# Moving score bounds, key sums and normalising products from VectorE to GpSimd, with paired value products and a changed release and load order

## The chip, the cores and the metric

The kernel runs on one core of a Trainium2 chip. The time is the device time of one execution in microseconds, as a median over several runs.

Five engines run at once, each through its own instructions in a fixed order: TensorE (PE in the profile, PEld for its weight loads), VectorE (DVE), ScalarE (ACT), GpSimd (POOL) and the sync engine (SP), which issues most DMAs.

## The reference

Two attention blocks on separate inputs of 2048 rows and width 512, 32 heads of 16, side by side in the output. Part A is softmax attention with one key and value head for all query heads. Part B is linear attention with softmax features.

```python
# A
q, k, v = x @ wq, x @ wk, x @ wv              # k and v: one head of 16
p = softmax(q_h @ k.T / 4)                    # 32 heads, 2048 x 2048
a = (p @ v) @ wo
# B
q, k, v = split(x @ wqkv)
phi = lambda t: concat(softmax(t @ w_phi), softmax(-(t @ w_phi)))
kv, z = phi(k).T @ v, phi(k).sum(rows)
b = ((phi(q) @ kv) / (phi(q) @ z + 1e-6)) @ wo
out = concat(a, b)
```

## The kernel before

Part A has 32 steps of four heads, and in each 16 tiles of keys. The exponential of a group of four 128x512 score tiles is made in one of two ways. ScalarE makes it exactly, two or three tiles at a time. Or VectorE makes it from the bits of a float16: it reads four score tiles from PSUM into int16 (`bits`, here "reads"), then adds a constant to the whole quad three times (`shift`), and TensorE sums four weighted versions. Such a quad costs VectorE four reads and three shifts.

```python
def bits():                                   # PSUM -> int16 in SBUF, 512 columns
    v.tensor_scalar(out=o, in0=ps[:, bank, :], scalar1=self.Z1, scalar2=self.Z0, op0=ALU.mult, op1=ALU.add)
def shift(t):                                 # SBUF -> SBUF, 2048 columns
    v.tensor_scalar(out=Z[:, t], in0=Z[:, 0], scalar1=256.0 * t, scalar2=None, op0=ALU.add)
```

The instructions stand in an order that a list scheduler in the kernel's own Python made when it was built. It keeps a model clock for each engine and picks the job that can start first, then by priority. On the chip that order is fixed: an engine that waits for one instruction does not go on to the next.

```python
job(("ss", st), "dve", 1.14, self.b_ssum, after=[("fe", st)], prio=1.9)          # key sums, part B
job(("on", sc), "dve", 0.60, ... finish_sc3(sc) ..., prio=1.3, after=[("rc", sc)] ...)  # normalising product, part A
job(("aq", ch), "dve", 0.60, ... absmax(QA[ch % 3]) ..., after=[("qa", ch)], prio=6)  # score bound
# (further jobs left out)
```

At the head of the kernel the sync queue is given all loads, the six transposes of part B first, then the bulk loads. It issues in order, so the first step's denominator copies (`finish_sc`, from `accS` to `denC`) stand behind all of them:

```python
for i in (1, 0): la = S.dma1(... dma_start_transpose(wT[i]) ..., deps=[la])
for c in range(4): la = self.load_xT(self.B_x, self.BxT, c, "BxT", la)
# then Bwv, Bwo, wo_pad (8 DMAs), wphi (8 DMAs); only then jobs
```

## Time and profile before

| | before |
|---|---|
| median of 3 runs | 816.45 us (814.57 to 816.78) |
| profiled run, span of its instructions | 809.98 us, 806.9 us |
| ScalarE busy | 748.5 us, 93% |
| TensorE busy | 733.9 us, 91% |
| VectorE busy | 722.3 us, 90% |
| GpSimd busy | 16.7 us, 2% |

The page's first part: each engine's busy time, its share of the span, and instructions.

```profile
span 806.9 us, 17313 instructions
PE 733.9 (91%) x7345; PEld 243.7 (30%) x7420; DVE 722.3 (90%) x1254; ACT 748.5 (93%) x690; POOL 16.7 (2%) x49
```

Three engines are nearly full, so the average does not name one limit. Three stretches do. The view by windows gives for each stretch the busy time of PE, PEld, DVE, ACT and POOL (instructions in brackets), then the granted TensorE clock, the DMA share and GB/s.

```profile
40.00:60.00 20.00, 10.35 (x103) 2.92 (x96) 10.55 (x19) 11.62 (x10) 0.00 (x0) 0.84 0.71 133
80.00:400.00 320.00, 294.64 (x3204) 97.82 (x3231) 311.50 (x538) 312.36 (x297) 4.83 (x10) 0.99 0.11 9
767.00:807.00 40.00, 28.58 (x304) 8.87 (x305) 18.55 (x35) 22.60 (x22) 0.00 (x0) 0.90 0.11 20
```

Between 80 and 400 us ScalarE works 312 of 320 us. Between 40 and 60 us it works 11.6 of 20, and so do the others: a hole. The last 40 us are half empty too. The timeline shows the hole (start, duration, engine, line, operation; in square brackets the idle time before it and what ended that):

```profile
44.92 0.68 DVE L1410 COPY f_accS<-f_ps 128x512 f32<-128x512 f32 x1
46.47 3.78 SPq L1465 DMA_DIRECT2D f_wo_pad<-in_A_wo_dram  x8
50.37 3.63 SPq L1487 DMA_DIRECT2D f_wphi<-in_B_w_phi_dram  x8
54.04 3.28 SPq L1801 DMA_DIRECT2D f_denC<-f_accS  x4
58.91 0.25 DVE L1809 RECIPROCAL f_denC<-f_denC 128x16 f32<-128x16 f32 x1 [8.52 <-DMA f_denC<-f_accS]
61.56 1.45 ACT L1653 ACTIVATE f_PT<-f_ps 128x1536 bf16<-128x1536 f32 x1 [8.52 <-PE f_ps L1598]
```

The accumulator was copied by 45.6 us, its denominators were fetched only at 54.0, because the queue was still issuing bulk loads. VectorE stood 8.5 us at the reciprocal, and in-order TensorE and ScalarE stood behind it.

The costliest groups (line, engine, operation, out<-in, shapes, count; busy us, mean ns of one; idle us before them and what ended it):

```profile
L1653 ACT ACTIVATE f_PT<-f_ps 128x1536 bf16<-128x1536 f32 (+1 forms) x621 | 721.4, 1264 | 45.3 <-PE f_ps L1598 42.1
L1745 DVE TENSOR_SCALAR f_Z<-f_ps 128x512 int16<-128x512 f32 x496 | 324.1, 682 | 34.9 <-PE f_ps L1598 34.3
L1758 DVE TENSOR_SCALAR f_Z<-f_Z 128x2048 int16<-128x2048 int16 x372 | 244.5, 685 | 0.7
```

The last two lines belong together. A shift handles 2048 columns in 685 ns, a read of PSUM 512 columns in 682. The shift runs at four times the rate.

### The profile page before, as it was taken

The page shows a single profiled execution, that of the slowest core. Times are in us where ns is not written, and L with a number is a line of the kernel's source. Part 1 is how long each engine was busy: PE and PEld are TensorE (multiplying, and loading weights), DVE is VectorE, ACT ScalarE, POOL GpSimd, SP SyncE. Part 2 cuts the span into 40 slices and gives each one's busy share as a digit, 9 for nine tenths or more (in the row PEclk, how much of TensorE's full clock was granted, in tenths as well). Part 3 has the DMA queues.
Part 4 walks back from the last instruction along what each step waited for, and adds up shares of the span by engine and source line. Part 5 has one row for each costly group of instructions (what it writes and reads, how often), then busy time and mean ns, then how long its engine had stood idle before and what let it go on. Part 6 is the DMA issues. An engine that isn't in the chain of part 4 may idle for free.

```text
span 806.9 us, 17313 instructions
## 1 busy us (share of the span) xinstructions
PE 733.9 (91%) x7345; PEld 243.7 (30%) x7420; DVE 722.3 (90%) x1254; ACT 748.5 (93%) x690; POOL 16.7 (2%) x49
## 2 busy tenths in 40 slices
PE   8959998988999999899999999999999999999894
PEld 2212322322323333323333233333333233333331
DVE  3759999999999999989899958999979999999962
ACT  4858999999999999999999998999999999999983
POOL 5000000000000000100000000000000000000000
PEclk9788999999999999999999998999999999999997
DMA  6561111101111101110101111011111101111110
GB/s 132 108 129 8 7 9 9 9 2 8 9 9 21 22 2 8 9 8 7 9 9 20 17 19 8 16 14 21 7 15 15 22 9 14 21 14 21 19 11 30
DMA packets 45179, 17.10 MB, mean 21 GB/s; under 512 B 37092, under 2 KB 43236, under 8 KB 45096
## 3 DMA queue, kind: packets, MB, share of 16 engines
q1 hardware_dynamic: 45096, 15.93, 15.8%
q8 instruction: 60, 0.98, 0.5%
q14 instruction: 23, 0.19, 0.1%
HBM read 2.15 MB, written 4.19 MB: 8 GB/s over the span
## 4 chain that ended last, share of the span: by engine, by line
DVE 63%; PE 25%; DMA 5%; ACT 2%; SPq 2%; issue 2%; DVEq 0%
DVE f_Z L1745 27%; DVE f_Z L1758 19%; PE f_ps L1598 8%; PE f_ps L1783 5%; PE f_ps L1695 4%; DMA f_AxT<-in_A_x_dram 2%; DVE f_vS L2041 2%; PE f_ps L2092 2%; ACT f_PT L1653 2%; DVE f_ssum L2015 2%; DVE f_accS L1410 2%; DMA f_BxT<-in_B_x_dram 2%; DVE f_On L1826 2%; PE f_ps L1839 2%; DVE f_Wk L2152 2%
## 5 line engine op out<-in xcount | busy, mean ns | idle before, releaser
L1653 ACT ACTIVATE f_PT<-f_ps 128x1536 bf16<-128x1536 f32 (+1 forms) x621 | 721.4, 1264 | 45.3 <-PE f_ps L1598 42.1
L1745 DVE TENSOR_SCALAR f_Z<-f_ps 128x512 int16<-128x512 f32 x496 | 324.1, 682 | 34.9 <-PE f_ps L1598 34.3
L1598 PE MATMUL f_ps<-f_QA,f_KR 32*128 32x512 bf16 x2048 | 315.6, 390 | 31.1 <-DVE f_Z L1745 20.8
L1758 DVE TENSOR_SCALAR f_Z<-f_Z 128x2048 int16<-128x2048 int16 x372 | 244.5, 685 | 0.7
L1598 PEld LDWEIGHTS f_ps<-f_QA,f_KR 32*128 32x128 bf16 x2048 | 80.3, 91 | 259.0 <-issue 85.7
L1695 PE MATMUL f_ps<-f_PT,f_VA 128*32 128x512 bf16 x1552 | 154.4, 395 | 2.6 <-DVE f_accS L1410 2.5
L1783 PE MATMUL f_ps<-f_Z,f_VK 128*32 128x512 f16 x1984 | 132.4, 388 | 3.3 <-DVE f_Z L1758 1.6
L1695 PEld LDWEIGHTS f_ps<-f_PT,f_VA 128*32 128x32 bf16 x1552 | 38.5, 93 | 97.9 <-issue 85.6
L1404 PE MATMUL f_ps<-f_ones,f_zero 128*128 128x512 bf16 (+7 forms) x204 | 61.2, 361 | 2.1 <-POOL f_zero L1423 1.3
L1783 PEld LDWEIGHTS f_ps<-f_Z,f_VK 128*32 128x32 bf16 x1984 | 42.3, 96 | 64.1 <-DVE f_Z L1758 16.7
L2092 PE MATMUL f_ps<-f_BxT,f_Wq 128*128 128x512 bf16 x112 | 29.4, 380 | 3.3 <-issue 1.6
L1839 PE MATMUL f_ps<-f_wo_pad,f_On 128*128 128x512 bf16 x87 | 22.9, 381 | 2.3 <-issue 1.1
L2152 DVE TENSOR_TENSOR f_Wk<-f_ps,f_wq 128x512 bf16<-128x512 f32 x32 | 21.9, 684 | 3.0 <-PE f_ps L2141 2.9
L1404 PEld LDWEIGHTS f_ps<-f_ones,f_zero 128*128 128x128 bf16 (+2 forms) x204 | 15.9, 97 | 28.1 <-issue 17.2
L1826 DVE TENSOR_TENSOR f_On<-f_accS,f_denS 128x512 bf16<-128x512 f32 x31 | 21.1, 682 | 0.4 <-DMA f_denS<-f_denS 0.4
L1410 DVE COPY f_accS<-f_ps 128x512 f32<-128x512 f32 x31 | 21.2, 682 | 0.2 <-PE f_ps L1695 0.2
L2041 DVE TENSOR_TENSOR f_vS<-f_ps,f_rs 128x1024 bf16<-128x1024 f32 x16 | 19.5, 1220 | 1.2 <-PE f_ps L2031 1.1
L2099 ACT ACTIVATE f_ET<-f_ps 128x512 bf16<-128x512 f32 x32 | 20.2, 636 | 0.4 <-PE f_ps L2092 0.4
L2015 DVE TENSOR_REDUCE f_ssum<-f_Ek 128x64 f32<-128x1024 bf16 x16 | 19.4, 1214 | 0.1
L1550 DVE TENSOR_SCALAR f_KR<-f_ps,f_half 128x512 bf16<-128x512 f32 x8 | 5.6, 745 | 15.1 <-PE f_ps L1542 15.1
L1588 PE MATMUL f_ps<-f_AxT,f_wq 128*128 128x512 bf16 x50 | 14.0, 393 | 4.7 <-DVE f_Z L1745 2.6
L2009 ACT ACTIVATE f_Ek<-f_ps 128x512 bf16<-128x512 f32 x32 | 17.8, 626 | 0.0
(95 smaller groups left out, 314.9 us busy)
## 6 DMA issues: line engine op xcount, KB each, us to landing
f_denS<-f_denS SPq DMA_DIRECT2D x124, 30.0 KB, 3.0
out_dram<-f_outB SPq DMA_DIRECT2D x18, 128.0 KB, 1.9
f_denC<-f_accS SPq DMA_DIRECT2D x124, 2.0 KB, 1.7
f_denS<-f_denC SPq DMA_DIRECT2D x124, 2.0 KB, 1.7
out_dram<-f_outA SPq DMA_DIRECT2D x14, 128.0 KB, 1.8
f_wq<-in_A_wq_dram SPq DMA_DIRECT2D x1, 512.0 KB, 4.2
f_Bwv<-in_B_wqkv_dram SPq DMA_DIRECT2D x1, 512.0 KB, 4.6
f_Bwo<-in_B_wo_dram SPq DMA_DIRECT2D x1, 512.0 KB, 6.8
```

The costliest lines, as they stand in the source:

```text
L1404: mm = pe.matmul(ps[0:m, bank, 0:n].rearrange("p (a n) -> p a n", n=128), lhsT=zero[0:r, 0:m], rhs=rhs, start=start, stop=start, **kw)
L1410: self.add("dve", lambda v: v.tensor_copy(out=out, in_=in_), reads=reads, writes=writes)
L1598: return pe.matmul(self.ps[:, bank, :], lhsT=self.KR[32 * g:32 * g + 32, sc % 2, kap * 128:(kap + 1) * 128], rhs=self.QA[32 * g:32 * g + 3 ...
L1653: self.add("act", lambda a: a.activation(out=PT[:, sl[0]:sl[0] + size, :], in_=ps[:, b0:b0 + size, :], func=ACT.Exp), reads=[("PS", b0 + i ...
L1695: mm = pe.matmul(ps[32 * g:32 * g + 32, bank, :], lhsT=w, rhs=PT[:, slots[g], :], start=start, stop=stop, tile_position=(0, 32 * g))
L1745: self.add("dve", lambda v: v.tensor_scalar(out=o, in0=ps[:, bank, :], scalar1=self.Z1, scalar2=self.Z0, op0=ALU.mult, op1=ALU.add), reads ...
L1758: self.add("dve", lambda v: v.tensor_scalar(out=Z[:, t], in0=Z[:, 0], scalar1=256.0 * t, scalar2=None, op0=ALU.add), reads=zk, writes=[("Z ...
L1783: mm = pe.matmul(ps[32 * g:32 * g + 32, bank, :], lhsT=w[:, k, :], rhs=Zf[:, k, sl[g], :], start=start and k == 0, stop=stop and k == 3, t ...
L1826: self.add("dve", lambda v: v.tensor_tensor(out=On[:, sc % 12, :], in0=accS[:, r, :], in1=R[:, r, :], op=ALU.mult), reads=[("accS", r), (" ...
L1839: mm = pe.matmul(ps[:, bank, :], lhsT=On[:, (8 * qc + a) % 12, q0:q0 + 128], rhs=self.wo_pad[:, a, :], start=(a == 0), stop=(a == 7))
L2092: mm = pe.matmul(ps[:, bank, :], lhsT=w[:, dc].rearrange("p x h a f -> p (x h a f)")[:, G * 128:G * 128 + 128], rhs=xT[:, dc, m * 512:(m + ...
L2152: self.add("dve", lambda v: v.tensor_tensor(out=o, in0=i, in1=w.unsqueeze(3).to_broadcast([128, 2, 16, 16]), op=ALU.mult), reads=[("PS", b ...
```

## The change

Its intent: VectorE is one of three full engines and GpSimd is idle, so give GpSimd work. Because the two engines may disturb each other, a GpSimd operation is released by the last shift of a VectorE quad (the key `lk`), and the scheduler starts it within 2 us of that. Besides: value products of ScalarE's groups run in pairs so that TensorE changes its tiling mode less often, with a higher limit of waiting groups (`HIGH` 13 to 16); the last step may take more VectorE quads (`LAST` 4, where `AHEAD`, 6, held before); the third shift of a quad now stands behind the first two; the six transposes of part B become jobs on the sync queue; two of the last four stores go to another queue. The diff, cut to its core:

```diff
-            job(("aq", ch), "dve", 0.60, ... absmax(QA ...) ...)
+            for i in range(2):      # sum of squares: product, then running sum
+                job(("aq", ch, i), "pool", 1.27, ... absmax_q(ch, i) ..., prio=6, ...)
-            job(("on", sc), "dve", 0.60, ... finish_sc3(sc) ...)
+            job(("on", sc), "pool" if sc < 29 else "dve", 1.25 if sc < 29 else 0.60, ...)
-            job(("ss", st), "dve", 1.14, self.b_ssum, after=[("fe", st)], prio=1.9)
+            for i, d in enumerate((1.27, 1.30)):      # a tree: 512, then 256, 128, 64 results
+                job(("ss", st, i), "pool", d, self.b_ssum, ...)
 # in ready(): start within LOCK of the last shift
+        if j.eng == "pool" and j.name != "kvfin" and self.asc < 32:
+            t = max(t, self.lk_from)
+            if t > self.lk_from + self.LOCK:
+                return None
 # in shift(t): the third one releases GpSimd, which reads "lk"
-                         reads=zk, writes=[("Zt", p, t)])
+                         reads=zk, writes=[("Zt", p, t)] + (["lk"] if t == 3 else []))
 # pairs of value products
-                             ok=... self.acc_ok(sc) ...
+                             ok=... self.acc_ok(sc) and self.pair(sc, q) ...
-            if j.name[0] == "pv" and self.nu - 4 * self.pvq > self.HIGH:
-                p = 0.5
+            if j.name[0] == "pv" and (self.nu - 4 * self.pvq > self.HIGH or (self.mode == "col" and j.name[1] == self.second)):
+                p = 0.5 if self.mode != "col" else 0.0
-    HIGH = 13
+    HIGH = 16
+    LOCK = 2.0
+    LAST = 4
 # late transposes
+        for i in range(6):
+            self.job(("ld", i), "sp", 0.1, ... load_late(i) ..., rel=26.0 + 5.6 * i)
 # (the third shift's dependency, buffers shared to make room, the flag's arithmetic, the stores' queue: left out)
```

More of the change, by code (lines that the diff above doesn't have):

```diff
@@ L1198, in __init__ @@
         self.wq = sb("wq", [128, 4, 512], BF)
-        self.wk_raw = sb("wk_raw", [128, 4, 16], BF)
         self.wk_rep = sb("wk_rep", [128, 4, 128], BF)
@@ L1216, in __init__ @@
         self.outA = sb("outA", [128, 2, 512], BF)
-        self.mq = sb("mq", [128, 20], F32)
+        self.mq = sb("mq", [128, 4], F32)
+        self.QM = sb("QM", [128, 512], BF)
         self.mqk = sb("mqk", [128, 4], F32)
@@ L1245, in __init__ @@
         self.wT = self.ET[:, 0:8, :]
+        self.wk_raw = self.ssum.rearrange("p a n -> p (a n)").bitcast(BF)[:, 0:64].rearrange("p (c n) -> p c n", c=4)
         self.mrow = self.Bwv[0:1, 0:2, :].rearrange("p a n -> p (a n)").bitcast(F32).rearrange("p (x c) -> p x c", c=4)
@@ L1256, in __init__ @@
         self.issued, self.waiting, self.njobs = set(), {}, 0
-        self.cand = dict(pe=[], act=[], dve=[], pool=[])
-        self.te = dict(pe=0.0, act=0.0, dve=0.0, pool=0.0)
+        self.cand = dict(pe=[], act=[], dve=[], pool=[], sp=[])
+        self.te = dict(pe=0.0, act=0.0, dve=0.0, pool=0.0, sp=0.0)
         self.bk, self.pe_hist, self.log = {}, [], []
         self.mode = None
+        self.lk_from = 0.0
         self.tile_end, self.row_free, self.row_next = [0.0] * 4, 0.0, set()
         self.open = False
-    TAIL = dict(pe=0.17, act=0.10, dve=0.09, pool=0.1)
+    TAIL = dict(pe=0.17, act=0.10, dve=0.09, pool=0.1, sp=0.0)
     SEM = 0.05
@@ L1407, in fill, with load_late @@
         self.add("pe", fn, reads=["ones", "zero"], **kw2)
+    def load_late(self, i):
+        if i < 2:
+            w = 1 - i
+            dst, key = self.wT[:, 4 * w:4 * w + 4, :], ("wT", w)
+            src = self.B_wqkv[:, 512 * w:512 * w + 512]
+        else:
+            c = i - 2
+            dst, key = self.BxT[:, :, c * 512:(c + 1) * 512], ("BxT", c)
+            src = self.B_x[0][c * 512:(c + 1) * 512, :]
+        src = src.rearrange("s (c d) -> s c d", c=4)
+        if self.rec is None:
+            self.lastT = self.S.dma1(lambda q: q.dma_start_transpose(out=dst, in_=src), writes=[key], deps=[self.lastT])
+            self.tw[key] = (self.fin + 5.6, "sp")
     def copy(self, out, in_, reads, writes):
@@ L1425, in head @@
             self.fill(start=True)
-        S.dma1(lambda q: q.dma_start(self.wk_raw, self.A_wk.rearrange("(c p) n -> p c n", p=128)), writes=["wk_raw"])
+        S.dma1(lambda q: q.dma_start(self.wk_raw, self.A_wk.rearrange("(c p) n -> p c n", p=128)), writes=["wk_raw", ("ssum", 0)])
         last = self.load_xT(self.A_x, self.xT, 0, "AxT", None)
@@ L1433, in head @@
             last = self.load_xT(self.A_x, self.xT, c, "AxT", last)
+        self.lastT = last
         add("pool", lambda g: g.memset(half[:, 0:1], 0.0), writes=["half0"])
@@ L1447, in head @@
         add("pool", lambda g: g.memset(self.bmx, 0.0), writes=["bmx"])
+        add("pool", lambda g: g.memset(self.QM, 0.0), writes=["QM"])
         if True:
-            la = last
-            for i in (1, 0):
-                src = self.B_wqkv[:, 512 * i:512 * i + 512].rearrange("s (c d) -> s c d", c=4)
-                la = S.dma1((lambda s_, i: (lambda q: q.dma_start_transpose(out=self.wT[:, 4 * i:4 * i + 4, :], in_=s_)))(src, i), writes=[("wT", i)], deps=[la])
-            for c in range(4):
-                la = self.load_xT(self.B_x, self.BxT, c, "BxT", la)
             S.batch_begin("sp")
@@ L1488, in head @@
             S.batch_end()
+        for i in range(6):
+            self.job(("ld", i), "sp", 0.1, (lambda i: (lambda: self.load_late(i)))(i), after=[("ld", i - 1)] if i else [], rel=26.0 + 5.6 * i)
         for k, t in (("wk_rep", 3.5), ("half1", 3.0), ("wv", 8.2), ("wq", 8.2), ("VA1", 5.0), ("ones", 1.0), ("zero", 1.0), ("bmx", 14.0)):
@@ L1495, in head @@
             self.tw["AxT", c] = (5.9 + 5.6 * c, "sp")
-            self.tw["BxT", c] = (39.0 + 5.6 * c, "sp")
         for k in ("Bwv", "Bwo", "wo_pad", "wo_pad0", "wphi", "wphi0", "ident", "mask0", "bok", ("Ss", 0), ("Ss", 1)):
             self.tw[k] = (66.0, "sp")
-        self.tw["wT", 1], self.tw["wT", 0] = (28.0, "sp"), (33.6, "sp")
     def jobs_a(self):
@@ L1509, in jobs_a @@
                     frees=[("pk", kc)] if e else [], prio=u + 0.2 * e)
-            job(("aK", kc), "dve", 0.60, (lambda kc: (lambda: self.absmax(self.KR[:, 0, kc * 512:kc * 512 + 512], kc, [("KR", 0, kc)])))(kc), after=[("KR", 0, kc)], prio=6)
+            job(("aK", kc), "dve", 0.60, (lambda kc: (lambda: self.absmax_k(kc)))(kc), after=[("KR", 0, kc)], prio=6)
             job(("pva", kc), "pe", 0.50, (lambda kc: (lambda: self.proj_va(kc)))(kc), after=[("pq", 0), ("pk", kc)], mode="full", nb=1, prio=u + 0.5)
@@ L1517, in jobs_a @@
             job(("qa", ch), "dve", 0.60, (lambda ch: (lambda: self.proj_q2(ch)))(ch), after=[("pq", ch)], frees=[("pq", ch)], prio=1)
-            job(("aq", ch), "dve", 0.60, (lambda ch: (lambda: self.absmax(self.QA[:, ch % 3, :], 4 + ch, [("QA", ch % 3)])))(ch), after=[("qa", ch)], prio=6)
+            for i in range(2):
+                job(("aq", ch, i), "pool", 1.27, (lambda ch, i: (lambda: self.absmax_q(ch, i)))(ch, i), prio=6,
+                    after=[("aq", ch, 0)] if i else [("qa", ch)] + [("pk", k) for k in range(4)] + ([("aq", ch - 1, 1)] if ch else []))
         for qt in range(12):
@@ L1531, in jobs_a @@
             job(("rc", sc), "dve", 0.18, (lambda sc: (lambda: self.finish_sc2(sc)))(sc), after=[("ac", sc)], prio=1.1)
-            job(("on", sc), "dve", 0.60, (lambda sc: (lambda: self.finish_sc3(sc)))(sc), prio=1.3,
+            job(("on", sc), "pool" if sc < 29 else "dve", 1.25 if sc < 29 else 0.60, (lambda sc: (lambda: self.finish_sc3(sc)))(sc), prio=1.3,
                 after=[("rc", sc)] + ([("op", 4 * ((sc - 12) // 8) + i, (sc - 12) % 8 // 4) for i in range(4)] if sc >= 12 else []))
@@ L1551, in proj_k2, with absmax_k, absmax_q @@
                  reads=[("PS", bank), "half1"] + [("half", g) for g in range(4)], writes=[("KR", e, kc)])
-    def absmax(self, src, col, reads):
-        self.add("dve", lambda v: v.tensor_reduce(out=self.mq[:, col:col + 1], in_=src, axis=AX.X, op=ALU.max, apply_absolute_value=True),
-                 reads=reads, writes=[("mq", col)])
+    def absmax_k(self, kc):
+        self.add("dve", lambda v: v.tensor_reduce(out=self.mq[:, kc:kc + 1], in_=self.KR[:, 0, kc * 512:kc * 512 + 512], axis=AX.X, op=ALU.max, apply_absolute_value=True),
+                 reads=[("KR", 0, kc)], writes=[("mq", kc)])
+    def absmax_q(self, ch, i):
+        QM, sq = self.QM, self.wk_rep.rearrange("p a n -> p (a n)")
+        a, b, o, key = (self.QA[:, ch % 3, :], self.QA[:, ch % 3, :], sq, "wk_rep") if i == 0 else (sq, QM, QM, "QM")
+        self.add("pool", lambda g: g.tensor_tensor(out=o, in0=a, in1=b, op=ALU.add if i else ALU.mult),
+                 reads=["wk_rep", "QM", "lk"] if i else [("QA", ch % 3), "lk"], writes=[key])
     def proj_va(self, kc):
@@ L1663, in expo, with pair @@
                              after=[("va", self.aquads[q][1] // 4)] + ([("pv", q - 1)] if q else []),
-                             ok=(lambda sc: (lambda: self.acc_ok(sc)))(self.aquads[q][0]))
+                             ok=(lambda sc, q: (lambda: self.acc_ok(sc) and self.pair(sc, q)))(self.aquads[q][0], q))
+                    self.qdone = q + 1
+    def pair(self, sc, q):
+        if self.qdone > q + 1 or self.nu - 4 * self.pvq > self.HIGH or q == self.second:
+            return True
+        return self.asc == 32 or (q + 1 < len(self.aquads) and self.aquads[q + 1][0] != sc)
     def acc_ok(self, sc):
@@ L1700, in pv @@
             self.pvq += 1
+            self.second = None if self.second == q else q + 1
     def dve_quad(self):
         for sc in (self.asc, self.asc + 1):
-            if sc < 32 and ("qa", sc // 2) in self.issued and 16 - self.at[sc] - self.dt[sc] >= self.AHEAD and all(("KR", sc % 2, k) in self.issued for k in range(4)):
+            if sc < 32 and ("qa", sc // 2) in self.issued and 16 - self.at[sc] - self.dt[sc] >= (self.AHEAD if sc < 31 else self.LAST) and all(("KR", sc % 2, k) in self.issued for k in range(4)):
                 return sc
@@ L1758, in go @@
                 self.add("dve", lambda v: v.tensor_scalar(out=Z[:, t], in0=Z[:, 0], scalar1=256.0 * t, scalar2=None, op0=ALU.add),
-                         reads=zk, writes=[("Zt", p, t)])
+                         reads=zk, writes=[("Zt", p, t)] + (["lk"] if t == 3 else []))
                 if self.rec is None:
                     self.dbusy -= 0.6
+                    if t == 3:
+                        self.lk_from = self.te["dve"]
             return go
         for t in range(1, 4):
-            self.job(("dS", quad, t), "dve", 0.60, shift(t), after=[("dz", k - x) for x in range(4)], prio=2)
+            self.job(("dS", quad, t), "dve", 0.60, shift(t), after=[("dz", k - x) for x in range(4)] if t < 3 else [("dS", quad, 1), ("dS", quad, 2)], prio=2)
         self.job(("dpv", quad), "pe", 0.87, lambda: self.d_pv(quad), mode="col", prio=1.4,
@@ L1825, in finish_sc3 @@
         accS, R, On = self.accS, self.denS, self.On
-        self.add("dve", lambda v: v.tensor_tensor(out=On[:, sc % 12, :], in0=accS[:, r, :], in1=R[:, r, :], op=ALU.mult),
-                 reads=[("accS", r), ("denS", r), ("row", r)], writes=[("On", sc % 12)])
+        self.add("pool" if sc < 29 else "dve", lambda v: v.tensor_tensor(out=On[:, sc % 12, :], in0=accS[:, r, :], in1=R[:, r, :], op=ALU.mult),
+                 reads=[("accS", r), ("denS", r), ("row", r), "lk"], writes=[("On", sc % 12)])
     def outproj(self, qt, half):
@@ L1897, in finish_last @@
             dst = self.out[0, (12 + i) * 128:(13 + i) * 128, 0:512]
-            self.S.dma1((lambda o, dst: (lambda q: q.dma_start(dst, o)))(o, dst), reads=[key], is_output=True)
+            self.S.dma1((lambda o, dst: (lambda q: q.dma_start(dst, o)))(o, dst), reads=[key], is_output=True, queue="act" if i % 2 else "sp")
     def flag_calc(self):
@@ L1902, in flag_calc @@
         mqk = self.mqk
-        for k, (src, rd) in enumerate(((self.mq[:, 4:20], [("mq", c) for c in range(4, 20)]), (self.mq[:, 0:4], [("mq", c) for c in range(4)]), (self.bmx, ["bmx"]),
+        for k, (src, rd) in enumerate(((self.QM, ["QM"]), (self.mq[:, 0:4], [("mq", c) for c in range(4)]), (self.bmx, ["bmx"]),
                                        (self.bok, ["bok"]))):
@@ L1913, in flag_calc2 @@
         add("dve", lambda v: v.tensor_reduce(out=m2, in_=self.mrow.rearrange("o p c -> o c p"), axis=AX.X, op=ALU.max), reads=["mrow"], writes=["m2"])
-        add("dve", lambda v: v.tensor_scalar(out=m2[:, 0:1], in0=m2[:, 0:1], scalar1=m2[:, 1:2], scalar2=16.0 / self.BOUND, op0=ALU.mult, op1=ALU.mult),
-            reads=["m2"], writes=["m2"])
+        for c in (1.0, 1.1 * (16.0 / self.BOUND) ** 2):
+            add("dve", (lambda c: (lambda v: v.tensor_scalar(out=m2[:, 0:1], in0=m2[:, 0:1], scalar1=m2[:, 1:2], scalar2=c, op0=ALU.mult, op1=ALU.mult)))(c),
+                reads=["m2"], writes=["m2"])
         add("dve", lambda v: v.tensor_scalar(out=m2[:, 2:3], in0=m2[:, 2:3], scalar1=1e-16, scalar2=None, op0=ALU.mult), reads=["m2"], writes=["m2"])
@@ L1943, in jobs_b @@
             job(("fe", st), "act", 1.08, self.b_ek, after=[("bk", st)], frees=[("bk", st)], prio=0)
-            job(("ss", st), "dve", 1.14, self.b_ssum, after=[("fe", st)], prio=1.9)
-            job(("rs", st), "dve", 0.75, self.b_rs, after=[("ss", st)], prio=1.9)
+            for i, d in enumerate((1.27, 1.30)):
+                job(("ss", st, i), "pool", d, self.b_ssum, after=[("ss", st, 0)] if i else [("fe", st)], prio=1.9)
+            job(("rs", st), "dve", 0.75, self.b_rs, after=[("ss", st, 1)], prio=1.9)
             job(("bv", st), "pe", 0.87, self.b_projv, after=[("fe", st)], mode="full", nb=1, prio=3)
@@ L2010, in b_ek, with b_ssum @@
                      reads=[("PS", bank)], writes=[("Ek", r, a)])
-    def b_ssum(self, st):
+    def b_ssum(self, st, i):
         r = st % 2
-        Ek, ssum = self.Ek, self.ssum
-        self.add("dve", lambda v: v.tensor_reduce(out=ssum[:, r, :], in_=Ek[:, r].rearrange("p h a f -> p (h a) f"), axis=AX.X, op=ALU.add),
-                 reads=[("Ek", r, 0), ("Ek", r, 1)], writes=[("ssum", r)])
+        x = self.Ek[:, r].rearrange("p h a f -> p (h a) f")
+        t = self.ET[:, 8:12, :].rearrange("p a n -> p (a n)").bitcast(F32)
+        y = [t[:, 0:512].rearrange("p (h f) -> p h f", f=8), t[:, 512:768].rearrange("p (h f) -> p h f", f=4), t[:, 768:896].rearrange("p (h f) -> p h f", f=2),
+             self.ssum[:, r, :].unsqueeze(2)]
+        tk = [("ET", 8 + k) for k in range(4)]
+        src, rd = (x, [("Ek", r, 0), ("Ek", r, 1)]) if i == 0 else (y[0], tk)
+        for k in ((0,) if i == 0 else (1, 2, 3)):
+            n = 8 >> k
+            self.add("pool", (lambda k, n, src: (lambda g: g.tensor_tensor(out=y[k], in0=src[:, :, 0:n], in1=src[:, :, n:2 * n], op=ALU.add)))(k, n, src),
+                     reads=rd + ["lk"], writes=tk if k < 3 else [("ssum", r)])
+            src, rd = y[k], tk
     def b_rs(self, st):
@@ L2206, in plan @@
         self.qleft, self.ndone = [64] * 32, [0] * 32
-        self.pvq = self.dpvq = self.dn = 0
+        self.pvq = self.dpvq = self.dn = self.qdone = self.second = 0
         self.dbusy, self.dz_out, self.row_tiles = 0.0, 0, {}
@@ L2211, in plan @@
         self.jobs_b(*self.T_B)
-        self.job("flag1", "dve", 0.8, self.flag_calc, after=[("aq", ch) for ch in range(16)] + [("aK", k) for k in range(4)] + [("rs", 15), ("qw", 3, 0)], prio=7)
-        self.job("flag2", "dve", 1.4, lambda: self.flag_calc2(flag), after=["flag1"], prio=7)
+        self.job("flag1", "dve", 1.4, self.flag_calc, after=[("aq", 15, 1)] + [("aK", k) for k in range(4)] + [("rs", 15), ("qw", 3, 0)], prio=7)
+        self.job("flag2", "dve", 1.6, lambda: self.flag_calc2(flag), after=["flag1"], prio=7)
         self.next_qk(0)
```

## The prediction

> **What bounds it now.** Three engines near their limit. The page gives ACT 748.5 us busy of 806.9, PE 733.9, DVE 722.3. By windows, from 60 to 780 us ACT is busy 697.5 of 720 (97%), DVE 680, PE 670; the chain of waits lies 63% on VectorE, nearly all in the two halves of its exponentials (496 PSUM reads, 324.1 us; 372 shifts, 244.5 us). TensorE issues in order: a late VectorE bank holds up ScalarE's scores. From 51 to 60 us everything stops: VectorE waits 8.5 us, once, for the first denominator's copy, ScalarE 8.5 and TensorE 9.1 behind it. The accumulator was ready at 45.6 us, but the sync queue, in order, was issuing transposes (to 45.3) and the bulk loads behind them (to 54.0).
>
> **What changes.** Instruction order of both builds:
> 1. VectorE loses 16 bounds (10.8 us), 16 key sums (19.4) and 29 of 31 normalising products (19.7): 50 us. The scheduler reinvests in 6 more VectorE quads (124 to 130): 24 reads at 0.65 and 18 shifts at 0.66, 27.5 us. Net -22 us.
> 2. ScalarE loses 24 tiles, 621 to 611 instructions. At 721.4/1552 = 0.465 us a tile: -11 us.
> 3. TensorE: quads add 96 and remove 24 matmuls; pairing the value products cuts changes of tiling mode (filler left out) from about 1196 to 1017. I estimate 0.1 us for each from the issue gaps, so 10 to 18 us, as slack.
> 4. The sync queue issues bulk loads first and spreads the six transposes; the first denominator's copy now stands before the second B transpose. That removes the hole: -8 us, all critical.
> 5. Two of four last stores move to the ACT queue: about -1 us.
>
> **What it adds.** GpSimd goes from 17 to about 130 us (estimate from its trace: 0.53 us for 128 columns, 0.61 for a 512-column copy, so 1.2 to 1.8 us for a 512-column product). "SBUF — State Buffer" of the Trainium skill, under who interferes with whom, says VectorE's two-port modes and GpSimd take a shared port pair exclusively. The shift qualifies: 2048 columns in 685 ns against 682 for 512 from PSUM. No run yet shows the collision. In the new order a shift often stands zero to two PSUM reads (0 to 1.2 us) after the releasing one, less than a GpSimd operation lasts. I expect about 100 collisions of 0.2 to 0.5 us, and some waits of VectorE for late key sums: 20 to 40 us of VectorE time, which eats most of its relief.
>
> **Sum.** Hole -8, tail -1, steady stretch -11 from ScalarE, -3 from less blocking, +6 returned by collisions: -17. Predicted 799 us, range 788 to 810. Chances: faster 0.53, same 0.44, slower 0.03.
>
> **What would show it.** (a) Windows: ScalarE near 20 of 20 us between 40 and 60, no 8 us wait for the denominator. (b) ScalarE's exponentials near 710 us; VectorE busy near 700 plus stretched shifts. (c) Mean shift above 0.685 us, or VectorE gaps beside GpSimd operations. (d) VectorE waiting for GpSimd's sums: total under 15 us. (e) ScalarE's busy share at 95 to 98% after the head.
>
> **What would make it wrong.** GpSimd products near 2 us or blocked twice, so key sums and normalised tiles come late and stall VectorE and TensorE in order: then only the hole is won, 805 to 812. Or bulk loads delay the last A transpose. Or collisions cost nothing and fewer mode changes free TensorE: 788.

## The result and the profile after

The changed kernel took 846.77 us (median of 4 runs, 843.87 to 849.92), the kernel before 815.79 beside it. The ratio is 1.038, 95% interval 1.034 to 1.042: slower. A ratio here is the mean time of one kernel's fast runs over the mean of the other's in the same rounds, so it isn't quite the ratio of the medians. Executions over 1.5% slower than the fastest of the same kernel are left out of the means.

The page's first part and windows of the changed kernel. The last window again begins with the last accumulator copy of part A.

```profile
span 842.1 us, 17654 instructions
PE 745.6 (89%) x7444; PEld 247.3 (29%) x7512; DVE 728.8 (87%) x1236; ACT 742.9 (88%) x680; POOL 144.0 (17%) x175
```

```profile
40.00:60.00 20.00, 18.20 (x171) 5.45 (x171) 19.66 (x32) 17.60 (x16) 6.93 (x6) 0.93 0.22 36
80.00:400.00 320.00, 282.31 (x3048) 91.61 (x3077) 300.90 (x506) 290.36 (x272) 82.87 (x94) 0.96 0.11 9
785.00:842.10 57.10, 37.93 (x358) 14.11 (x359) 25.85 (x46) 21.52 (x21) 0.00 (x0) 0.79 0.11 23
```

The hole is gone: ScalarE works 17.6 us between 40 and 60. But between 80 and 400 us it works 290 of 320 us in place of 312, and the last stretch is 57 us long in place of 40. VectorE's busy time did not fall by 22 us, it rose by 6.

The 31 accumulator copies of part A mark its progress and split both traces in three:

| stretch | before | after | difference |
|---|---|---|---|
| start to second copy | 76.7 | 67.2 | -9.5 |
| second copy to last copy | 690.5 | 718.0 | +27.5 |
| last copy to end | 39.8 | 56.9 | +17.1 |
| span | 806.9 | 842.1 | +35.1 |

The profiled run of before (810.0 us) was 0.8% below its median, so not all of the 35 us is the change. By the ratio it is some 31 us.

The groups that answer to those of before, and one of GpSimd's:

```profile
L1680 ACT ACTIVATE f_PT<-f_ps 128x1536 bf16<-128x1536 f32 x611 | 714.0, 1251 | 64.0 <-PE f_ps L1625 59.1
L1780 DVE TENSOR_SCALAR f_Z<-f_ps 128x512 int16<-128x512 f32 x520 | 335.8, 679 | 45.3 <-PE f_ps L1625 45.0
L1793 DVE TENSOR_SCALAR f_Z<-f_Z 128x2048 int16<-128x2048 int16 x390 | 277.5, 739 | 0.7
L1864 POOL TENSOR_TENSOR f_On<-f_accS,f_denS 128x512 bf16<-128x512 f32 x29 | 39.0, 1345 | 387.5 <-DVE f_Z L1793 357.3
```

The read of PSUM took 679 ns, as before. The shift went from 685 to 739 ns in the mean. Sorted by whether a GpSimd operation ran at the same time, 318 shifts took 681 ns and 72 took 994 ns, the longest 1757. The excess over 690 ns sums to 22.2 us. The reads do not care: 108 of them beside GpSimd took 680 ns. The timeline of two collisions:

```profile
131.91 2.25 DVE L1793 TENSOR_SCALAR f_Z<-f_Z 128x2048 int16<-128x2048 int16 x2
132.30 1.31 POOL L2063 TENSOR_TENSOR f_ET<-f_Ek 128x512 f32<-128x512 bf16 x1 [8.68 <-ACT f_Ek L2049]
133.75 1.53 POOL L1864 TENSOR_TENSOR f_On<-f_accS,f_denS 128x512 bf16<-128x512 f32 x1
```

```profile
487.05 2.96 DVE L1793 TENSOR_SCALAR f_Z<-f_Z 128x2048 int16<-128x2048 int16 x3
487.87 1.58 POOL L1864 TENSOR_TENSOR f_On<-f_accS,f_denS 128x512 bf16<-128x512 f32 x1 [24.60 <-DVE f_Z L1793]
```

In the first, two shifts take 2.25 us where two took 1.28 before: the second began at 132.5, 0.2 us after a GpSimd operation that ran to 133.6, and ended at 134.2, some 0.55 us later. The next GpSimd operation, begun before that, was stretched in its turn (1.53 us; undisturbed ones of its form take 1.27). In the second, three shifts take 2.96 us. The waiting counts as busy time of VectorE, not as idle time. This is the port pair that the Trainium skill describes in "SBUF — State Buffer", under who interferes with whom: the engine that starts first holds it for its whole instruction and the other is blocked. This trace agrees, 994 against 681 ns, and it agrees with the page that an instruction with at most one SBUF input outside the two-port modes is not touched (680 ns).

Only few waits for GpSimd are idle time (waiter, what ended the wait: total us, times, longest):

```profile
DVE f_bmx L2070 <- POOL f_ssum L2063: 6.0, 7, 2.8
```

And the tail, with part B's last stages one behind the other after the attention's last exponential at 809.4 us:

```profile
814.97 0.69 DVE L2201 TENSOR_TENSOR f_Wk<-f_ps,f_wq 128x512 bf16<-128x512 f32 x1 [0.70 <-PE f_ps L2190]
816.12 1.49 PE L2231 MATMUL f_ps<-f_Bwo,f_oT 128*128 128x512 bf16 x3 [1.19 <-DVE f_Wk L2201]
817.71 0.69 DVE L1431 CAST f_outB<-f_ps 128x512 bf16<-128x512 f32 x1 [2.05 <-PE f_ps L2231]
819.10 0.38 ACT L1913 ACTIVATE f_ET<-f_ps 128x256 f32<-128x256 f32 x1 [9.69 <-PE f_ps L2190]
825.06 0.69 DVE L1431 CAST f_outB<-f_ps 128x512 bf16<-128x512 f32 x1 [2.05 <-PE f_ps L2231]
829.62 0.69 DVE L1431 CAST f_outB<-f_ps 128x512 bf16<-128x512 f32 x1 [2.05 <-PE f_ps L2231]
```

The last copy of part B's output stands at 829.6 us. Before it stood at 765, ahead of the end of part A:

```profile
764.71 0.68 DVE L1410 CAST f_outB<-f_ps 128x512 bf16<-128x512 f32 x1
```

In the changed kernel each step of the tail waits for the one before it, on engines that are otherwise empty.

This tail could have been seen without a chip. In the built instruction order of the changed kernel 16 of the last-stage products, 24 of the turning products and 20 of the query products of part B stand behind the last score. In the kernel before there are none.

### The profile page after: what moved, and what is told of

The parts are those of the page before. It is cut to its first block, busy times and chain, and to the rows that moved or that the text cites. A ratio compares the mean times of both kernels' runs of the same rounds, so it can differ in the third digit from the quotient of the medians.

```text
span 842.1 us, 17654 instructions
## 1 busy us (share of the span) xinstructions
PE 745.6 (89%) x7444; PEld 247.3 (29%) x7512; DVE 728.8 (87%) x1236; ACT 742.9 (88%) x680; POOL 144.0 (17%) x175
## 3 DMA queue, kind: packets, MB, share of 16 engines
q1 hardware_dynamic: 44808, 15.67, 15.2%
## 4 chain that ended last, share of the span: by engine, by line
DVE 62%; PE 28%; ACT 4%; POOL 2%; issue 1%; DMA 1%; SPq 1%; DVEq 0%; POOLq 0%
DVE f_Z L1780 27%; DVE f_Z L1793 22%; PE f_ps L1625 8%; PE f_ps L1820 6%; PE f_ps L1729 4%; ACT f_PT L1680 3%; DVE f_Wk L2201 2%; PE f_ps L2141 2%; PE f_ps L1410 2%; DVE f_accS L1431 2%; POOL f_ET L2063 1%; DVE f_vS L2090 1%; PE f_ps L2231 1%; DVE f_QA L1431 1%; PE f_ps L1877 1%
## 5 line engine op out<-in xcount | busy, mean ns | idle before, releaser
L1680 ACT ACTIVATE f_PT<-f_ps 128x1536 bf16<-128x1536 f32 x611 | 714.0, 1251 | 64.0 <-PE f_ps L1625 59.1
L1780 DVE TENSOR_SCALAR f_Z<-f_ps 128x512 int16<-128x512 f32 x520 | 335.8, 679 | 45.3 <-PE f_ps L1625 45.0
L1793 DVE TENSOR_SCALAR f_Z<-f_Z 128x2048 int16<-128x2048 int16 x390 | 277.5, 739 | 0.7
L1864 POOL TENSOR_TENSOR f_On<-f_accS,f_denS 128x512 bf16<-128x512 f32 x29 | 39.0, 1345 | 387.5 <-DVE f_Z L1793 357.3
L1410 PE MATMUL f_ps<-f_ones,f_zero 128*128 128x512 bf16 (+8 forms) x224 | 65.1, 355 | 1.9 <-POOL f_zero L1444 1.3
L1729 PEld LDWEIGHTS f_ps<-f_PT,f_VA 128*32 128x32 bf16 x1528 | 37.2, 94 | 94.8 <-issue 69.5
L2063 POOL TENSOR_TENSOR f_ET<-f_Ek 128x512 f32<-128x512 bf16 x16 | 21.1, 1321 | 94.7 <-DVE f_Z L1793 74.7
L1581 POOL TENSOR_TENSOR f_wk_rep<-f_QA 128x512 bf16<-128x512 bf16 x16 | 17.7, 1104 | 83.8 <-DVE f_Z L1793 54.3
L1581 POOL TENSOR_TENSOR f_QM<-f_wk_rep,f_QM 128x512 bf16<-128x512 bf16 x16 | 20.2, 1265 | 26.3 <-DVE f_Z L1793 25.7
L2063 POOL TENSOR_TENSOR f_ET<-f_ET 128x256 f32<-128x256 f32 (+1 forms) x32 | 22.0, 688 | 8.3 <-DVE f_Z L1793 6.1
L2231 PE MATMUL f_ps<-f_Bwo,f_oT 128*128 128x512 bf16 x58 | 17.6, 428 | 4.1 <-DVE f_Wk L2201 2.0
```

The lines of the kernel that those rows point to most:

```text
L1410: mm = pe.matmul(ps[0:m, bank, 0:n].rearrange("p (a n) -> p a n", n=128), lhsT=zero[0:r, 0:m], rhs=rhs, start=start, stop=start, **kw)
L1680: self.add("act", lambda a: a.activation(out=PT[:, sl[0]:sl[0] + size, :], in_=ps[:, b0:b0 + size, :], func=ACT.Exp), reads=[("PS", b0 + i ...
L1729: mm = pe.matmul(ps[32 * g:32 * g + 32, bank, :], lhsT=w, rhs=PT[:, slots[g], :], start=start, stop=stop, tile_position=(0, 32 * g))
L1780: self.add("dve", lambda v: v.tensor_scalar(out=o, in0=ps[:, bank, :], scalar1=self.Z1, scalar2=self.Z0, op0=ALU.mult, op1=ALU.add), reads ...
L1793: self.add("dve", lambda v: v.tensor_scalar(out=Z[:, t], in0=Z[:, 0], scalar1=256.0 * t, scalar2=None, op0=ALU.add), reads=zk, writes=[("Z ...
L1864: self.add("pool" if sc < 29 else "dve", lambda v: v.tensor_tensor(out=On[:, sc % 12, :], in0=accS[:, r, :], in1=R[:, r, :], op=ALU.mult), ...
```

## The experiments

Two theories at first. Theory C: GpSimd's time itself is the loss, through collisions and late results. Theory O: the new order is the loss, part B pushed behind the attention. Stretches are given as in the table above (start, steady, tail). The profiled runs come from chips whose PSUM reads took 677 to 691 ns, so steady stretches of different runs compare only to about 1%, while the tails repeat within 1 us. Verdicts use the ratios to the kernel before. A hundredth of the ratio is about 8.2 us.

### 1. Same order, GpSimd's operations made tiny

```diff
-  g.tensor_tensor(out=o, in0=a, in1=b, ...)                                   # bounds
+  g.tensor_tensor(out=o[:, 0:8], in0=a[:, 0:8], in1=b[:, 0:8], ...)
-  g.tensor_tensor(out=y[k], in0=src[:, :, 0:n], in1=src[:, :, n:2 * n], ...)  # key sums
+  g.tensor_tensor(out=y[k][:, 0:2, 0:1], in0=src[:, 0:2, 0:1], in1=src[:, 0:2, n:n + 1], ...)
-  v.tensor_tensor(out=On[:, sc % 12, :], ...)                                 # products, sc < 29
+  v.tensor_tensor(out=On[:, sc % 12, 0:8], ...)
+  # the targets are set to constants at the head
```

> The changed kernel with every instruction in the same order on every engine, but GpSimd's moved operations cut to 8 columns or 2 elements (a wrong result on purpose). It takes GpSimd's time away and leaves the order. If collisions on the shared port and late GpSimd results are the whole loss (theory C), it comes to about 842 - 22 (stretched shifts) - 6 (waits for key sums) and less, below 800 us once the hole and ScalarE's 11 us are counted. If the order is to blame (theory O: value products in pairs and GpSimd's release windows push part B behind the attention), the stretch from the last accumulator copy to the end stays near 57 us (before: 40) and the total is 815 to 825.

Ratio 1.010 (1.005 to 1.015), 818.4 us; the result is wrong, as meant. The instruction order of TensorE, VectorE, ScalarE and the sync queue was compared with the changed kernel's and is the same. Stretches 64.0, 694.4, 56.5. The groups of shift and exponential:

```profile
L1796 DVE TENSOR_SCALAR f_Z<-f_Z 128x2048 int16<-128x2048 int16 x390 | 258.1, 693 | 0.7
L1683 ACT ACTIVATE f_PT<-f_ps 128x1536 bf16<-128x1536 f32 x611 | 710.4, 1254 | 41.2 <-PE f_ps L1628 37.7
```

Both theories were half right. GpSimd's time is worth 2.8 hundredths, 23 us. ScalarE's idle time before its exponentials falls from 64.0 to 41.2 us, the same 23 us, and most of it ended with a score of TensorE (59.1 and 37.7 us). That fits stretched shifts that reach ScalarE by way of TensorE. What stays is the tail, 56.5 us. The granted clock is no good rival: between 80 and 400 us it was 0.96 in the changed kernel and 0.98 here, but also 0.96 and 0.97 in runs 4 and 10, which lost nothing.

The second reading is worth as much. Here VectorE is relieved of 50 us at no price at all, and the kernel is still slower than before. The tail and the pairs weigh on this run too; run 12 takes them out.

### 2. Everything back on VectorE, the rest of the change kept

```diff
-  job(("aq", ch, i), "pool", ...); job(("on", sc), "pool" if sc < 29 ...); job(("ss", st, i), "pool", ...)
+  job(("aq", ch), "dve", 0.60, ...); job(("on", sc), "dve", 0.60, ...); job(("ss", st), "dve", 1.14, ...)
```

> The changed kernel with bounds, key sums and normalising products back on VectorE; pairs, the higher limit and the late loads stay. Theory C: no collisions, so 800 to 806 us. Theory O: in its order 16 of the last-stage products (12 of s8) still stand behind the last score, so a tail of 50 us or more and 815 to 825 us.

Ratio 1.014 (1.009 to 1.019), 822.9 us; stretches 62.9, 700.1, 56.1. Theory O's expectation held. No GpSimd work, and the tail is there. GpSimd's work does not make it. Run 3 shows that pairs and limit do.

### 3. No pairs, old limit, GpSimd keeps its work

```diff
-  ok=... self.acc_ok(sc) and self.pair(sc, q) ...
+  ok=... self.acc_ok(sc) ...
-  (... > self.HIGH or (self.mode == "col" and j.name[1] == self.second)): p = 0.5 if self.mode != "col" else 0.0
+  ... > self.HIGH: p = 0.5
-    HIGH = 16
+    HIGH = 13
```

> The changed kernel without pairs and with the old limit of 13; GpSimd keeps its work. Its order leaves no part B behind the last score and has 122 VectorE quads. Theory C: collisions as in the changed kernel (about 70 shifts near 1.0 us), total 825 or more. Theory O: tail back to 40 us, total 810 to 818.

Ratio 1.025 (1.018 to 1.032), 830.6 us; stretches 69.5, 719.6, 40.3. The tail is gone and the steady stretch is as long as in the changed kernel: 67 shifts beside GpSimd took 962 ns. Theory C's part alone. Only pairs and limit differ from the changed kernel, and they are worth 1.3 hundredths here; the two intervals do not overlap (1.018 to 1.032, 1.034 to 1.042).

### 4. Late loads alone

```diff
-  la = S.dma1(... transposes of B at the head ...)
+  self.job(("ld", i), "sp", 0.1, ... load_late(i) ..., rel=26.0 + 5.6 * i)
   # and two of the last stores on the ACT queue; VectorE, pairs and limit as before
```

> The kernel before with the late transposes and the two-queue last stores alone (124 quads, no pairs, nothing on GpSimd). Both theories: the 8.5 us hole goes, 805 to 809 us, so a ratio of 0.987 to 0.991. If the hole was harmless slack that returns elsewhere: 813 to 816.

Ratio 0.990 (0.984 to 0.996), 805.4 us. The reciprocal that waited 8.5 us no longer waits. Run 10 repeats it with more rounds.

### 5. to 7. One part of GpSimd's work made tiny at a time, same order

The edit is that of run 1, for one of the three parts.

> Same order as the changed kernel on every engine but GpSimd's; only the key sums are cut to 2 elements (a wrong result on purpose), bounds and products stay whole. With all three cut the ratio to the kernel before was 1.010, with none 1.038. Theory C (each collision on the shared port goes straight into the time): of 23 us of stretched VectorE operations about 9 lie beside key sums, and 6 us of waits for them vanish, so the ratio is 1.020 to 1.027. Theory L (late results of GpSimd, not the port, cost the time): the sums are the only results that VectorE waits for, so this alone gives nearly all, 1.010 to 1.016.

> The same with only the normalising products cut to 8 columns. Theory C: about 6 of the 23 us of stretch, so a ratio of 1.028 to 1.034. Theory L: nothing in the trace waits for these products, 1.036 to 1.040.

> The same with only the score bounds cut to 8 columns. Nothing waits for the bounds before the end, so this tells the theories apart. Theory C: about 9 of the 23 us of stretch, so a ratio of 1.024 to 1.031. Theory L: 1.036 to 1.040.

A rival here was theory L: that late results cost the time, not the port.

| tiny part | ratio (95%) | stretch of VectorE operations | idle time of VectorE until GpSimd |
|---|---|---|---|
| none (changed kernel) | 1.038 (1.034 to 1.042) | 23.0 us | 6.0 us |
| key sums | 1.024 (1.017 to 1.030) | 16.8 | 2.3 |
| products | 1.024 (1.017 to 1.031) | 15.2 | 6.2 |
| bounds | 1.022 (1.016 to 1.028) | 15.0 | 5.0 |
| all three | 1.010 (1.005 to 1.015) | 0.5 | 0.9 |

(Stretch here: excess over the median of the same operation and form, where it is over 60 ns.) The products came out lower than theory C expected, 1.024 for 1.028 to 1.034, and so did the bounds, 1.022 for 1.024 to 1.031. But nothing waits for bounds or products within the steady stretch, and making either tiny gave as much as making the sums tiny. Theory L falls as the main cause. Three parts at 1.5 hundredths each would be 4.4, and all together gave 2.8. Each difference is uncertain by some 0.8, so whether the parts add is not settled.

### 8. Same order without the release

```diff
-  t = self.S.add(eng, fn, reads=reads, writes=writes, ...)
+  t = self.S.add(eng, fn, reads=[r for r in reads if r != "lk"], writes=[w for w in writes if w != "lk"], ...)
```

> The changed kernel with the same order, whole operations and a right result; only GpSimd's wait for the last shift is gone, it starts when its data is there. If the release helps as it was meant: more collisions and a ratio of 1.045 or more. If it only chooses which shift is hit: within 0.5 percent of 1.038, with some 70 shifts beside GpSimd again and 20 us of stretch. If the release makes GpSimd late and that hurts: 1.030 or less.

Ratio 1.044 (1.035 to 1.053), 848.8 us, right result, between two of its expectations; 86 shifts beside GpSimd at 989 ns, stretch 27.3 us. The release saves some 4 us of stretch, and its worth in time is not clear of noise. It does not keep the engines apart: in the built order of the changed kernel, in 26 of 64 releases, a shift of another quad stands directly behind the releasing instruction or one read after it. This run rules out another thing. In the changed kernel the last shift writes the key that GpSimd reads, so it must also wait for GpSimd's earlier operations. Without the key there is no such wait, and the stretch is still there.

### 9. GpSimd's operations in pieces

```diff
-  g.tensor_tensor(out=o, in0=a, in1=b, ...)
+  for c in range(0, 512, 128): g.tensor_tensor(out=o[:, c:c + 128], in0=a[:, c:c + 128], in1=b[:, c:c + 128], ...)
   # products and key sums likewise, 128 results each
```

> The changed kernel, same order, right result; every moved GpSimd operation is cut into pieces of 128 results, so it holds the port for at most about 0.45 us at a time in place of 1.1 to 1.3. If a shift waits for the running GpSimd instruction to end: the longest shift falls from 1.76 to about 1.1 us, the stretch from 22 to 8 to 14 us, ratio 1.022 to 1.032. If the port passes on without a chance for VectorE between pieces: longest shift 1.7 us or more and a ratio of 1.04 or more.

Ratio 1.052 (1.048 to 1.056), 855.7 us: a miss, and the most instructive one. The mechanism did what was expected. The longest shift fell from 1757 to 987 ns and the stretch from 23.0 to 10.7 us. Yet the time rose, by other lines:

```profile
L1794 DVE TENSOR_SCALAR f_Z<-f_Z 128x2048 int16<-128x2048 int16 x390 | 267.5, 714 | 12.5 <-POOL f_QM L1582 4.5 <-POOL f_ET L2068 3.0 <-POOL f_On L1867 2.2
```

```profile
DVE f_bmx L2075 <- POOL f_ssum L2068: 16.8, 9, 5.9
```

Each piece has its own overhead (0.46 us for 128 columns against 1.27 for 512), and GpSimd's busy time in the steady stretch rose from 123 to 184 us. Now VectorE is idle for late key sums (16.8 us), and its last shifts wait for the GpSimd operations of the release before (11.7 us), the wait named under run 8. Stretch and waits together were 29 us in the changed kernel and are 39 here. The rise of the ratio, 1.4 hundredths or 11 us, is of that size.

### 10. Late loads again, and the limit alone

Run `headonly5` is run 4 again, with more rounds. Run `limit16` is run 2 without pairs: late loads, everything on VectorE, `HIGH = 16`. From run 4 it differs in the limit and in two smaller points of the change: the third shift stands behind the first two, and the last step may take more quads (`LAST = 4` for 6).

> The late loads alone again, with more rounds, as the candidate that beats both kernels and as the base for the run beside it: 0.987 to 0.993 expected from the first time (0.990, interval 0.984 to 0.996). If the first time was luck: 0.995 or more.

> Late loads, everything on VectorE, limit 16 without pairs; its order leaves no part B behind the last score, 123 quads. With pairs and limit 16 the ratio was 1.014, with pairs and limit 13 it was 1.0075, with neither 0.990. If pairs alone cost the time: 0.987 to 0.996. If the limit costs as well: 0.998 or more, and the two add up.

Late loads alone: ratio 0.986 (0.981 to 0.992), just below what was expected, 803.9 us as the median of six of which one was slow, right result. This version beats both kernels: both its intervals lie below 1. Its window at the place of the hole (to be compared with the first window of before):

```profile
40.00:60.00 20.00, 18.24 (x177) 5.24 (x173) 18.26 (x32) 18.06 (x16) 0.00 (x0) 0.93 0.24 33
```

The limit alone: 0.997 (0.993 to 1.002), tail 35.3 us. It lands between its two expectations.

### 11. Pairs with the old limit

```diff
-    HIGH = 16
+    HIGH = 13
   # on run 2: pairs kept, everything on VectorE
```

> Pairs with the old limit of 13, late loads, everything on VectorE. Its order has no part B behind the last score (the same with limit 16 left 12 last-stage products there and had a tail of 56 us). If pairs and limit together make the tail, and pairs are otherwise neutral: tail 40 us, ratio 0.985 to 0.995, like the late loads alone (0.990). If fewer changes of tiling mode are worth what the prediction gave them: 0.980 or less. If pairs alone cost time: 1.00 or more.

Ratio 1.008 (1.003 to 1.012), 819.9 us, stretches 65.4, 709.9, 39.9. The tail is gone, as its order said. But the run is 1.8 to 2.1 hundredths above runs 4 and 10, although the changes of tiling mode fell from 1194 to 1049. With runs 4 and 2 and the limit alone this is a two by two, all on VectorE with late loads:

| | limit 13 | limit 16 |
|---|---|---|
| no pairs | 0.986 and 0.990 (runs 4 and 10) | 0.997, tail 35 us |
| pairs | 1.008, tail 40 us | 1.014, tail 56 us |

It isn't a clean one. The first field lacks the third shift's new place and `LAST = 4`, which the other three have, and no run separates these two. Clean are the right column and the lower row: at limit 16 pairs cost 1.7 hundredths, and with pairs the limit costs 0.6. At limit 16 the loss lies in the tail, as far as the two profiles tell (56.1 for 35.3 us; the steady stretch is 700.1 for 701.7). Only both together leave part B behind the attention.

### 12. No pairs, tiny GpSimd operations

The edit of run 1 on run 3; same order as run 3.

> The run without pairs, same order, but GpSimd's moved operations cut to 8 columns or 2 elements (a wrong result on purpose): what relieving VectorE of 50 us is worth at best, with no collisions and no tail. Without pairs and with whole operations the ratio was 1.025. If collisions cost here what they cost in the changed kernel (about 3 points): 0.990 to 1.000, so no better than the late loads alone (0.990), as VectorE's time is not what limits. If relief of VectorE does pay once nothing is given back: 0.975 or less.

Ratio 0.994 (0.990 to 0.999), 807.9 us; wrong result, as meant. Stretches 63.0, 697.9, 40.0. GpSimd's time is worth 3.1 hundredths here too. And with VectorE 50 us lighter, nothing given back, no tail and no hole, the kernel is no faster than with the late loads alone. (Its 122 quads leave ScalarE 8 more tiles than the 124 there, at 0.465 us some 4 us or half a hundredth, so the two are about equal.) In this order VectorE's time was not the limit. From run 1 this run differs in pairs and limit alone: without GpSimd's time they cost 1.6 hundredths, tail included.

### 13. Part B raised earlier in the changed kernel

```diff
-    AGE = 3.0
-    AGED = 0.8
+    AGE = 2.0
+    AGED = 0.2
```

> The changed kernel, pairs and limit 16 kept, where the scheduler raises a waiting part-B product sooner and higher (2 us and 0.2 in place of 3 us and 0.8). In its order no part B stands behind the last score; 122 VectorE quads. If the tail is a plain loss: tail 40 us and 822 to 834 us, ratio 1.010 to 1.024. If part B only moves its cost into the steady stretch: ratio 1.030 to 1.045. Collisions stay: some 70 shifts near 1.0 us.

Ratio 1.021 (1.017 to 1.026), 831.7 us, stretches 67.0, 731.7, 39.1 (its profiled run was the slowest of its five, with 837.9 us of span). The tail is a real loss of about 1.7 hundredths in the changed kernel, and a scheduler setting takes it back. 58 shifts still collide. Pairs and limit stay in this run, and it is no slower than run 3 without them (1.025, 1.018 to 1.032). By the traces it has 1057 changes of tiling mode for 1208 there. So pairs need not cost time, and 151 fewer changes brought no gain that is clear of noise. (The scheduler setting may help by itself; that was not run apart.)

## Why the prediction was wrong

The forecast was 799 us; 846.8 came. By the ratios the change splits so: late loads -1.0 to -1.4 hundredths; pairs, limit, the third shift's place and the last step's quads +2.4 to +2.8 (run 2 against runs 4 and 10), of which clean comparisons give pairs and limit 1.3 to 1.6 (runs 3 and 12); moving the work to GpSimd, if it took no time there, -0.4 (run 1 against run 2); GpSimd's time +2.8. The sum is +3.8 by construction, as each part starts at the run where the one before ended.

Two terms of the prediction's sum failed by most: "+6 returned by collisions", where about 23 us came, and "tail -1", where the tail grew by 17 (a net loss of some 14 us, by run 13).

- **The hole, -8 us: right.** Late loads alone gave 0.986 and 0.990, 8 to 11 us.
- **The tail, -1 us: wrong, it was +17.** The step took only the two stores into account. Part B's last stages stood behind the last score in the built order, which was there to be read before predicting.
- **Pairs, "10 to 18 us, as slack": no gain, and a loss in most orders.** Fewer changes of tiling mode were counted as time for TensorE. At limit 16, with everything on VectorE, pairs cost 1.7 hundredths, by way of the tail. In run 13, without the tail, they cost nothing that shows. That they hold back each first product until a second is there, or that they take the place of part B's products, is argued, not shown. The steady stretch of `pairs13` is longer than in runs 4 and 10 (709.9 for 699 us), and no single wait in its trace accounts for that.
- **"The scheduler reinvests in 6 more VectorE quads": the failed step of the main argument.** The count was right (130; it was read from the built order), and so was ScalarE's relief (714.0 us of exponentials; 710 was forecast). The cause was wrong. GpSimd relieves VectorE just as much in runs 3 and 13, and those have 122 quads. More than 124 stood only in orders that left part B for the tail (128 in run 2, 130 in the changed kernel). The 11 us taken from ScalarE were bought with a tail of 17.
- **Collisions, 100 of 0.2 to 0.5 us, 20 to 40 us of VectorE time: the mechanism was right and the size too** (72 shifts, 23 us of stretch and 6 us of waits). **"+6 returned": wrong.** About 23 us were returned, nearly all. VectorE had idle time, but not at the moments of the collisions: a late shift or read holds up in-order TensorE and through it ScalarE. Whether an engine has slack on average does not say that a delay on it is free.
- **"-3 from less blocking", and with it the reading of the chain of waits (63% on VectorE): wrong.** Run 12 takes 50 us from VectorE and, in its order, gains nothing over the late loads. The chain shows who came last in each small step, and three engines that are full within a few per cent take turns at that. Between 80 and 400 us ScalarE had 312 of 320 us, so there was little to win but by less work for ScalarE.
- **What would show it:** (b), (c) and (d) came as written (714.0 and 728.8 us; 739 ns; 6.0 us), and (a) nearly (17.6 of 20 us, and no wait for the denominator). (e) failed: ScalarE's share between 80 and 400 us was 91%, not 95 to 98. And nothing on the list looked at the end of the kernel.

What stays open: why the steady stretch is longer with pairs at limit 13, what the third shift's place and the last step's quads are worth, and why pairs with the higher limit push part B behind. All lie in the scheduler's choices, which these runs changed but did not dissect.

## What to carry to other kernels

Before work is moved off an engine, make the moved operations tiny: same order, wrong result, one run. It gives what the relief can bring in that order, before the scheduler uses the room for other work. In the two orders where it was tried (runs 1 and 12) the kernel was no faster than with the late loads alone. When idle GpSimd takes elementwise work beside fast SBUF-to-SBUF operations of VectorE, count each overlap of the two as time that the whole pipeline may pay, whatever VectorE's average slack. And where a scheduler fixes the order, read in the built order what stands behind the last step of the main loop before trusting a sum of busy times.

## What the Trainium skill lacked or had wrong

- "SBUF — State Buffer", who interferes with whom: agrees on the lock (994 against 681 ns for a shift beside GpSimd) and on what is not touched (PSUM reads 680 ns). It does not say where the wait shows: in this profile a blocked shift counts as busy (up to 1757 ns), so the idle time before the shifts stayed at 0.7 us.
- The same section: the cost beyond the blocked engine is not told. Here 23 us of stretch on VectorE brought 23 us more idle time on ScalarE, although VectorE was busy only 87% of the span.
- No page that was read tells that shorter GpSimd operations trade the lock for overhead: 128-column pieces cut the longest blocked shift from 1757 to 987 ns and the stretch from 23.0 to 10.7 us, yet the kernel went from 1.038 to 1.052.
- "GPSIMD Engine Reference", performance versus the Vector engine: its 2.6 cycles a column for two inputs at 1.2 GHz give, as an estimate, 1.11 us for 512 columns. The undisturbed operations here took 1.04 to 1.15 us in bf16 and 1.27 us in fp32, so the figure is good to about 15%.
- "Perfetto Trace Analysis" calls GpSimd's spans unreliable. Here spans of undisturbed operations of one form repeated within 20 ns (1267 to 1284 ns for the fp32 product), so that stretched ones could be told apart.
